# Fused attention and mixer on one Trainium2 core: third batch's query tails and fourth batch's queries loaded at other places of one queue

## The chip, the cores and the metric

The kernel runs on one core of a Trainium2 chip. A core has a matrix engine (PE; PEld is its weight load), a vector engine (DVE), an activation engine (ACT), a general engine (POOL) and an engine that mostly issues transfers (SP, SyncE), each with an instruction stream of its own that it works through in order. Sixteen DMA engines move data between HBM and the on-chip memory. The metric is the device time of one execution in microseconds (us), as the median of several runs.

## The reference

Eight batches of 8 heads, 576 positions, 64 elements a head. A linear attention with cosine and sine features is followed by a token and channel mixer:

```python
q_p = phi(q, cos_w, sin_w)          # relu(x)*cos, relu(x)*sin: 64 -> 128 features
k_p = phi(k, cos_w, sin_w)
kv = einsum('bhsf,bhsd->bhfd', k_p, v)
z = sum(k_p, axis=2)
num = einsum('bhsf,bhfd->bhsd', q_p, kv)
den = einsum('bhsf,bhf->bhs', q_p, z)[..., None] + 1e-06
x = (num / den), heads side by side: (8, 576, 512)
u = x + (relu(x^T @ w_tok1) @ w_tok2)^T      # over positions, 576 -> 256 -> 576
out = u + relu(u @ w_ch1) @ w_ch2            # over channels, 512 -> 1536 -> 512
```

## The kernel before

**Tiling.** The 576 positions of a batch are four chunks of 128 (0 to 3) and a tail of 64. The tails of two batches with numbers 2n and 2n+1 share one tile of 128 rows, called chunk R (its number is 4). Each batch loads three 1 MB tiles (qt, kt, vt, 128 partitions with 1 KB pieces) and tails qtt, ktt, vtt (128 KB each, 64 partitions, 256-byte pieces). For batch 2 the tails of batches 2 and 3 are both loaded, so that each of its tail tiles takes two transfers.

**Stages.** For each batch a `Front` makes the features (`k_side`, `q_side`, L263, on DVE), casts the values into v_aug (`values`, L274, on ACT), sums keys times values on PE (`kv`, L320) and copies the result out (`kv_out`, L331: one half on ACT, one on DVE, tile kv_sb). The query features are turned by a DMA transpose that SP issues (`q_trans_dma`, L350: qp to qpT, qp_tail to qpT_tail). `num` (L359) multiplies them with kv_sb; DVE divides (L367 to L369). The token mixer (`tok1` L382, `tok2` L406) gives u, which ACT casts (L413) and SP turns (L438, L443). A `Channel` then does the channel mixer: `c_main` (L546) and `c_tail` (L566) into h1T, `o_step` (L579) into the output tiles o_sb (L584), which SP stores (L586, L590).

**The order is written out by hand.** PE runs the steps of `Channel` of batch b one after the other: 12 steps for the channel matmuls (step 0 to 11), then the output steps, two matmuls each. Between them the work of batch b+1 is put at given steps: `pieces` returns a plan of (step, what, chunk). A negative step lies that many steps before the end of the loop before, among the last output steps there. What the plan puts there goes in that order into the streams of all engines. So the fronts of batches 2 and 3 are made in the loops of batches 1 and 2, and their pieces at negative steps at the end of the loops of batches 0 and 1.

**Loads.** `load_batch` puts transfers into SP's stream at the place where it is called: main tiles, tails, or both. All go through one SP queue, together with the stores and the transposes. An SP transfer waits, before it is issued, for the one eight places earlier to land, for its data, and for its buffer. kt, qt, vt and the tails have two buffers each.

The three flags of `pieces`: `first` is batch 1, `odd` are batches 1, 3, 5, 7, `late` is batch 2 alone. Lists that concern the change:

- batch 2: casts of the values at steps 6, 6, 7, 7, 7; K features of chunks 0 to 3 at -4, -3, 0, 1, Q features at 1, 2, 3, 4, K tail at 5, Q tail at 6; kv at 7, 7, 8, 8, 8 and kv_out at 8; num from step 10 on in the order 0, 1, 2, R, 3.
- batch 3, as odd: K and Q features of chunk 0 at -4 and -3, the others at steps 0 to 2; kv at 2 to 6, kv_out at 6, num from step 8 on. Its Q tail is the other half of batch 2's and is made with that.

SP's order before in the two stages (x2 is two transfers):

- batch 2: uT x2, uT_tail, vt(2), ktt x2, qtt x2, vtt x2, store x2, qpT 0 to 3, qpT_tail, kt(3), vt(3), qt(3), store x2
- batch 3: uT x2, kt(4), ktt x2, tail store x2, store, qpT 0, store, qpT 1 to 3, vt(4), vtt x2, qt(4), qtt x2

Of the kernel before, what the change touches and what calls it, by code (L numbers as in the profile page):

```python
# [16 lines left out]
def kernel(  # L17
# [17 lines left out]
    B, H, S, D = q.shape  # L35
# [11 lines left out]
    NCH = D_ch // P  # L47
# [30 lines left out]
    def after(later, earlier):  # L78
        tc.add_manual_dep(later.ins, earlier.ins.name,
                          mybir.DependencyInfo(mybir.DependencyClass.Sync,  # L80
                                               mybir.DependencyReason.DATA),
                          reason="order of the first loads")


    def load_main(dst, src, b, lo=0, hi=H, eng=nc.sync):
        return eng.dma_start(
            out=dst[:, lo:hi, 0:R * D].rearrange("p h (r d) -> p h r d", r=R),
            in_=src[b, lo:hi, 0:SM, :].rearrange("h (p r) d -> p h r d", r=R))


    def load_tail(dst, src, b, eng=nc.sync):
        return eng.dma_start(out=dst[half(b % 2)],
                                 in_=src[b, :, SM:S, :].rearrange("h s d -> s h d"))

    def tiles():
        return tuple(io.tile([P, H, R * D], F32, name=n) for n in ("qt", "vt", "kt"))

    def tail_tiles():
        return tuple(io.tile([P, H, D], F32, name=n) for n in ("qtt", "vtt", "ktt"))
# [116 lines left out]
    class Front:  # L216
# [244 lines left out]
        def pieces(self, b, before):  # L461

            first, odd, late = b == 1, b % 2 == 1, b == 2
            V, KV, N = self.values, self.kv, self.num
            KS, QS, QT, T = self.k_side, self.q_side, self.q_trans, self.tok2
            C, O = 0, NCH
            if first:

                u, act, pool = before.tok2, nc.scalar, nc.gpsimd
                plan = [(4, KS, 0), (4, KS, 1), (5, u, 0, ps_at, False), (5, KS, 2, True),
                        (6, KS, 3, True), (6, u, 1, ps_at, False), (7, KS, R), (7, V, R, nc.vector), (8, V, 0, act),
                        (8, V, 2, pool), (8, load_w_ch2, 0), (8, V, 3, pool),
                        (8, load_w_ch2, 1), (8, load_w_ch2, 2),
                        (8, u, 2, None, False), (9, V, 1, act), (9, u, 3, None, False),
                        (9, QS, 0), (10, u, R, None, False)]
                plan += [(11, KV, ci) for ci in range(NSC)]
                plan += [(11, QS, 1), (11, QS, 2), (11, self.kv_out),
                         (11, QT, 0, (0, H), act, ps_at), (11, QT, 1), (11, QS, R),  # L480
                         (O, QT, 2), (O, N, 0), (O, QS, 3), (O + 1, QT, R),
                         (O + 1, N, 1), (O + 3, N, 2), (O + 3, QT, 3),
                         (O + 5, N, R), (O + 7, N, 3), (O + 8, before.tail_cast)]
            else:
                plan = [(C + at, V, ci, nc.scalar)
                        for ci, at in enumerate((6, 6, 7, 7, 7) if late else (-1, -1, 0, 1, 2))]

                if odd:
                    sides = ((-4, KS, 0), (-3, QS, 0), (0, KS, 1), (0, KS, 2), (1, QS, 1),
                             (1, KS, 3), (1, QS, 2), (2, QS, 3))  # L490
                elif late:
                    sides = ((-4, KS, 0), (-3, KS, 1), (0, KS, 2), (1, KS, 3), (1, QS, 0),
                             (2, QS, 1), (3, QS, 2), (4, QS, 3), (5, KS, R), (6, QS, R))
                else:
                    sides = ((-4, KS, 0), (-3, KS, 1), (0, KS, 2), (1, KS, 3), (1, QS, 0),
                             (2, KS, R), (2, QS, 1), (3, QS, 2), (4, QS, R), (5, QS, 3))
                for at, side, ci in sides:
                    plan.append((C + at, side, ci))
                    if side == QS:
                        plan.append((C + at, self.q_trans_dma, ci))  # L500

                plan += [(C + at, KV, ci) for ci, at in
                         enumerate((7, 7, 8, 8, 8) if late else
                                   (2, 3, 4, 5, 6) if odd else (2, 3, 4, 6, 7))]
                plan.append((C + (8 if late else 6 if odd else 7), self.kv_out))
            if first:
                at, mix, t = (), O + 7, O + 11
            elif odd:
                at, mix, t = (C + 8, C + 9, C + 10, C + 11, O + 2), O + 3, O + 7
            elif late:  # L510
                at, mix, t = (C + 10, C + 11, O + 1, O + 2, O + 4), O + 5, O + 9
            else:
                at, mix, t = (C + 9, C + 10, C + 11, O + 1, O + 3), O + 4, O + 8
            plan += [(i, N, ci) for i, ci in zip(at, ORDER)]
            plan += [(mix, self.mix_head, 0), (mix + 1, self.mix_head, 1),
                     (mix + 2, self.mix_tail)]

            plan += [(t + at, T, ci) for ci, at in enumerate((0, 1, 2, 3, 3) if not first else
                                                             (0, 0, 1, 2, 2))]
            plan += [(t + 3 - first, self.u_trans_dma, 3, R)]  # L520
            plan.append((t + 2 - first, self.u_trans_dma, 0, 3))
            if odd:
                plan.append((t + 3 - first, self.tail_trans_dma))
            slots = {}
            for slot, what, *args in sorted(plan, key=lambda p: p[0]):
                slots.setdefault(slot, []).append((what, args))
            return slots
# [186 lines left out]
    def load_batch(b, which="kvq", behind=None, main=True, tails=True):  # L714
        if b not in io_tiles:
            io_tiles[b] = tiles()
        if b // 2 not in io_tails:
            io_tails[b // 2] = tail_tiles()
        qt, vt, kt = io_tiles[b]
        qtt, vtt, ktt = io_tails[b // 2]  # L720
        done = []
        for n in which:
            dst, tail_dst, src = {"k": (kt, ktt, k), "v": (vt, vtt, v), "q": (qt, qtt, q)}[n]
            if main:
                done.append(load_main(dst, src, b))
            if behind is not None and len(done) == 1:
                after(done[0], behind)
            if tails and b % 2 == 0:
                load_tail(tail_dst, src, b)
            if tails and (b % 2 == 0 or b == 1):  # L730
                load_tail(tail_dst, src, b | 1)
        return done
# [4 lines left out]
    tails = {0: tail0}  # L737
    fronts = {0: Front(0, results[0], tail0)}

    def next_front(b):  # L740
        if b // 2 not in tails:
            tails[b // 2] = Tail(b // 2)
        fronts[b] = Front(b, results[b], tails[b // 2])
        return fronts[b].pieces(b, fronts[b - 1])
# [3 lines left out]
    for b in range(B):  # L748
        if b > 0:
            c = Channel(b, results[b], tails[b // 2])  # L750
        steps = c.steps(AHEAD if b == 0 else 0)
        following = {}
        for i, step in enumerate(steps):
            step()
            for what, args in slots.pop(i, ()):
                what(*args)


            if b == 0 and i == NCH:
                load_batch(2, "kq", behind=w_ch2_done[1], tails=False)  # L760
            if b == 0 and i == NCH + 13:
                load_batch(2, "v", tails=False)
                load_batch(2, "kqv", main=False)
            if b == 1 and i == 9:
                load_batch(3, "kvq")
            if 1 < b < B - 2 and i == NSC:
                load_batch(b + 2, "vq")
            if 0 < b < B - 3 and i == NCH + 12:
                load_batch(b + 3, "k")
            if i == len(steps) - 4 and b + 2 < B:  # L770
                following = next_front(b + 2)
            for what, args in following.pop(i - len(steps), ()):
                what(*args)
        assert not slots
        slots = following
# [32 lines left out]
```

## Time and profile before

| what | value |
|---|---|
| median of 3 runs | 270.0 us (269.47 to 270.21) |
| the profiled execution, its own time | 270.61 us |
| its span, first to last instruction | 268.8 us |
| mean granted clock of PE | 1.000 |
| DMA | 53.68 MB in 91815 packets, mean 200 GB/s |
| qpT transposes, median from issue to landing | 4.3 us |
| qtt loads, median from issue to landing | 5.3 us |
| stores of 256 KB, median from issue to landing | 2.9 us |

The span leaves out 1.8 us around the program. Times in the timelines count from the start of the span; a row gives start and length in us, then engine, line and operation, the tiles as out<-in, and in square brackets the idle time of that engine before it with what ended it. SPq rows are issues: their length is how long SP was busy issuing, not how long the transfer took. A landing is the time at which the transfer's semaphore told of its end.

### The profile page before, as it was taken

How to read it: one execution, taken by the hardware profiler on the slowest of the kernel's cores; microseconds unless marked ns; L12 is line 12 of the kernel's file. 1: busy time of each engine (PE TensorE's matmuls, PEld its weight loads, DVE VectorE, ACT ScalarE, POOL GpSimd, SP SyncE). 2: the span in 40 equal slices, each digit the busy share in tenths (PEclk: the TensorE clock that was granted, in tenths of full speed). 3: DMA queues.
4: the chain of work that ended last, by engine and by line, in shares of the span. 5: the costliest groups of instructions: out<-in, count | busy, mean ns of one | idle time of the engine just before them, and what ended most of it. 6: DMA issues, size and time to landing. Idle time of an engine off the chain costs nothing.

```text
span 268.8 us, 5101 instructions
## 1 busy us (share of the span) xinstructions
PE 260.0 (97%) x2029; PEld 139.2 (52%) x2050; DVE 164.9 (61%) x376; ACT 129.9 (48%) x228; POOL 10.9 (4%) x24
## 2 busy tenths in 40 slices
PE   7989999999999999999999999999999999999994
PEld 2565465455544455446644455446644455445543
DVE  6874798794366747777466747776565846720022
ACT  4954975528606272446606372546606362526400
POOL 6300220000000000000000000000000000000000
PEclk9999999999999999999999999999999999999999
DMA  6999999589999999469984989189974580180032
GB/s 217 342 277 275 333 162 285 211 210 253 179 316 289 251 208 319 146 166 266 182 307 117 287 207 355 54 179 254 229 261 117 156 120 0 53 202 3 2 107 88
DMA packets 91815, 53.68 MB, mean 200 GB/s; under 512 B 59408, under 2 KB 86928, under 8 KB 91792
## 3 DMA queue, kind: packets, MB, share of 16 engines
q1 hardware_dynamic: 88432, 49.62, 69.5%
q0 software_dynamic: 2832, 3.21, 7.2%
q10 hardware_dynamic: 528, 0.52, 0.6%
q8 instruction: 16, 0.26, 0.4%
q14 instruction: 7, 0.06, 0.1%
HBM read 35.85 MB, written 9.44 MB: 168 GB/s over the span
## 4 chain that ended last, share of the span: by engine, by line
PE 86%; DVE 6%; DMA 3%; ACT 3%; issue 1%; DVEq 0%; ACTq 0%
PE o_ps L579 33%; PE c_ps L546 25%; PE u_ps L406 7%; PE b_ps L382 6%; PE ct_ps L566 3%; PE kv_ps L320 3%; PE num_ps L359 3%; DVE x_sb L369 3%; DMA qt<-in_q_dram 2%; DVE qp L263 1%; ACT h1T L550 1%; PE qT_ps L340 1%; DMA qpT_tail<-qp_tail 1%; PE idle_ps L204 1%; ACT v_aug L274 1%; PE c_ps L556 1%
## 5 line engine op out<-in xcount | busy, mean ns | idle before, releaser
L579 PE MATMUL o_ps<-w_ch,h1T 128*128 128x512 bf16 (+1 forms) x380 | 92.6, 372 | 0.6
L546 PE MATMUL c_ps<-uT,w_ch 128*128 128x512 bf16 (+2 forms) x384 | 92.2, 372 | 0.1
L550 ACT ACTIVATE h1T<-c_ps 128x512 bf16<-128x512 f32 x93 | 55.5, 599 | 60.5 <-PE c_ps L546 60.1
L579 PEld LDWEIGHTS <-h1T 128*128 128x128 bf16 x396 | 37.3, 98 | 39.5 <-issue 0.2
L546 PEld LDWEIGHTS <-w_ch 128*128 128x128 bf16 x384 | 33.5, 97 | 29.5 <-issue 0.2
L584 DVE TENSOR_TENSOR o_sb<-o_ps,u_sb 128x512 f32<-128x512 f32 (+1 forms) x33 | 22.3, 674 | 29.5 <-PE o_ps L579 29.4
L409 DVE TENSOR_TENSOR u_sb<-u_ps,x_sb 128x512 f32<-128x512 f32 x32 | 21.7, 689 | 6.0 <-PE u_ps L406 5.6
L413 ACT CAST u_bf<-u_sb 128x512 bf16<-128x512 f32 x28 | 17.3, 620 | 16.7 <-DVE u_sb L409 16.7
L406 PE MATMUL u_ps<-B,w_tok 128*128 128x512 bf16 x79 | 22.4, 379 | 0.2
L387 ACT ACTIVATE B<-b_ps 128x512 bf16<-128x512 f32 x8 | 4.8, 598 | 33.7 <-PE b_ps L382 33.5
L369 DVE TENSOR_TENSOR x_sb<-num_ps,den 128x512 bf16<-128x512 f32 x28 | 19.4, 691 | 1.0
L566 PEld LDWEIGHTS <-w_ch 128*128 128x128 bf16 x192 | 14.0, 98 | 9.2
L382 PE MATMUL b_ps<-x_sb,w_tok 128*128 128x512 bf16 x63 | 17.7, 379 | 0.1
L263 DVE TENSOR_SCALAR kp<-kt,cos_t 128x512 bf16<-128x512 f32 x32 | 15.2, 481 | 3.8 <-DMA kt<-in_k_dram 3.8
L566 PE MATMUL ct_ps<-uT_tail,w_ch 128*128 128x128 bf16 x192 | 17.2, 219 | 0.0
L274 ACT CAST v_aug<-vt 128x512 bf16<-128x512 f32 (+1 forms) x30 | 16.8, 587 | 0.1
L263 DVE TENSOR_SCALAR qp<-qt,cos_t 128x512 bf16<-128x512 f32 (+1 forms) x35 | 15.9, 455 | 0.5 <-DMA qt<-in_q_dram 0.5
L263 DVE TENSOR_SCALAR qp<-qt,sin_t 128x512 bf16<-128x512 f32 (+1 forms) x35 | 15.9, 455 | 0.0
L359 PEld LDWEIGHTS <-qpT 128*128 128x128 bf16 x256 | 11.5, 98 | 6.1 <-issue 1.1
L584 DVE TENSOR_TENSOR o_sb<-o_ps,u_tail 128x512 f32<-128x512 f32 x4 | 2.8, 692 | 19.0 <-PE o_ps L579 19.0
L359 PE MATMUL num_ps<-kv_sb,qpT 128*128 128x65 bf16 x256 | 13.0, 193 | 1.3 <-DVE x_sb L369 0.5
L331 DVE CAST kv_sb<-kv_ps 128x260 bf16<-128x260 f32 x8 | 3.5, 433 | 16.6 <-ACT kv_sb L331 16.5
(93 smaller groups left out, 228.6 us busy)
## 6 DMA issues: line engine op xcount, KB each, us to landing
out_dram<-o_sb SPq DMA_DIRECT2D x31, 256.0 KB, 2.9
kt<-in_k_dram SPq DMA_DIRECT2D x7, 1024.0 KB, 6.6
vt<-in_v_dram SPq DMA_DIRECT2D x7, 1024.0 KB, 6.6
qt<-in_q_dram SPq DMA_DIRECT2D x7, 1024.0 KB, 8.4
w_ch<-in_moe_w_ch_dram POOLq DMA_DIRECT2D x4, 384.0 KB, 10.2
w_ch<-in_moe_w_ch_dram POOLq DMA_DIRECT2D x3, 512.0 KB, 7.5
out_dram<-o_sb SPq DMA_DIRECT2D x10, 128.0 KB, 2.3
qtt<-in_q_dram SPq DMA_DIRECT2D x8, 128.0 KB, 5.3
```

Of the source, the lines that this page charges most:

```text
L263: nc.vector.tensor_scalar(o_ap, i_ap, scalar1=w, scalar2=0.0, op0=ALU.mult, op1=ALU.max)
L274: nc.scalar.copy(dst, src)
L359: nc.tensor.matmul(num_ps[:, g, j * DP:j * DP + D1], self.qT_of(ci, h), self.kv_sb[g][:, j, 0:D1], start=True, stop=True)
L369: nc.vector.tensor_mul(self.x_of(ci)[rows].rearrange("p (g j d) -> p g j d", g=2, j=HH), nv[:, :, :, 0:D], den.to_broadcast([rows.stop - r ...
L382: nc.tensor.matmul(self.b1_ps[mi], w, self.x_of(ci), start=(ci == ORDER[0]), stop=(ci == ORDER[-1]))
L406: nc.tensor.matmul(u_ps, w_tok2[:, ki, ci * P:(ci + 1) * P], self.B1[:, ki, :], start=(ki == 0), stop=(ki == NT - 1))
L409: nc.vector.tensor_add(u, u_ps[rows], self.x_of(ci)[rows])
L546: nc.tensor.matmul(c_ps[:, lo:hi], w_ch1[:, ki, mi * P:(mi + 1) * P], uT[:, lo // P:hi // P, ki, :], start=(ki == 0), stop=(ki == NCC - 1))
L550: nc.scalar.activation(self.h1T[:, mi, :], c_ps, AF.Relu)
L566: nc.tensor.matmul(self.ct_ps[:, mi % R, :], w_ch1[:, ki, mi * P:(mi + 1) * P], self.tail.uT[:, ki, :], start=(mi % R == 0 and ki == 0), s ...
L579: nc.tensor.matmul(o_ps, h, w_ch2[:, ki, cols], start=ki == 0, stop=ki == NCH - 1)
L584: nc.vector.tensor_add(o_sb, o_ps, u)
```

## The change

It moves loads and features; what is computed, and PE's order of instructions, stay the same.

1. Batch 2's casts of values stand at steps 5, 6, 6, 7, 7: those of chunks 0 and 2 are one step earlier.
2. Batch 2's late loads in the loop of batch 0 are vt, vtt, ktt; qtt moves to step 3 of the loop of batch 1, where it stands behind the transposes of batch 2's chunks 0 to 2.
3. Batch 3's qt is loaded near the end of the loop of batch 1, behind the transposes of batch 2's u, in the place where kt and ktt of batch 4 were; these move to step 1 of the loop of batch 2.
4. Batch 3 has a list of its own: K features of all chunks first (-4, -3, 0, 1), Q features with their transposes at steps 2, 3, 4, 5.

The last two lines of the diff keep the general rule for the later batches.

```diff
@@ -483,9 +483,12 @@
                          (O + 5, N, R), (O + 7, N, 3), (O + 8, before.tail_cast)]
             else:
                 plan = [(C + at, V, ci, nc.scalar)
-                        for ci, at in enumerate((6, 6, 7, 7, 7) if late else (-1, -1, 0, 1, 2))]
-
-                if odd:
+                        for ci, at in enumerate((5, 6, 6, 7, 7) if late else (-1, -1, 0, 1, 2))]
+
+                if b == 3:
+                    sides = ((-4, KS, 0), (-3, KS, 1), (0, KS, 2), (1, KS, 3),
+                             (2, QS, 0), (3, QS, 1), (4, QS, 2), (5, QS, 3))
+                elif odd:
                     sides = ((-4, KS, 0), (-3, QS, 0), (0, KS, 1), (0, KS, 2), (1, QS, 1),
                              (1, KS, 3), (1, QS, 2), (2, QS, 3))
                 elif late:
@@ -759,13 +762,19 @@
             if b == 0 and i == NCH:
                 load_batch(2, "kq", behind=w_ch2_done[1], tails=False)
             if b == 0 and i == NCH + 13:
-                load_batch(2, "v", tails=False)
-                load_batch(2, "kqv", main=False)
+                load_batch(2, "v")
+                load_batch(2, "k", main=False)
+            if b == 1 and i == 3:
+                load_batch(2, "q", main=False)
             if b == 1 and i == 9:
-                load_batch(3, "kvq")
+                load_batch(3, "kv")
+            if b == 1 and i == NCH + 12:
+                load_batch(3, "q")
+            if b == 2 and i == 1:
+                load_batch(4, "k")
             if 1 < b < B - 2 and i == NSC:
                 load_batch(b + 2, "vq")
-            if 0 < b < B - 3 and i == NCH + 12:
+            if 1 < b < B - 3 and i == NCH + 12:
                 load_batch(b + 3, "k")
             if i == len(steps) - 4 and b + 2 < B:
                 following = next_front(b + 2)
```

SP's order after, in the two stages:

- batch 2: uT x2, uT_tail, vt(2), vtt x2, ktt x2, store x2, qpT 0 to 2, qtt x2, qpT 3, qpT_tail, kt(3), vt(3), store x2
- batch 3: uT x2, qt(3), tail store x2, store x2, kt(4), ktt x2, qpT 0 to 3, vt(4), vtt x2, qt(4), qtt x2

On DVE the order in batch 2 is unchanged. In batch 3 it was K0, Q0, K1, K2, Q1, K3, Q2, Q3 (two instructions each) and becomes K0 to K3, Q0 to Q3. On ACT the casts of chunks 0 and 2 of batch 2 come one h1T earlier.

## The prediction

> **What bounds the kernel now.** I began with the page: TensorE (PE) is busy for nearly the whole span, so time can only come out of its pauses.
>
> ```profile
> PE 260.0 (97%) x2029; PEld 139.2 (52%) x2050; DVE 164.9 (61%) x376; ACT 129.9 (48%) x228; POOL 10.9 (4%) x24
> ```
>
> The step from one 128x512 matmul to the next is 216 ns. Going through the PE records for steps that are longer than their form's usual one, I find, behind the first 28 us and apart from single lost records, only the stretch from 59 to 75 us, where batch 2 is prepared between batch 1's channel matmuls. Its timeline on PE (start, length, engine, line):
>
> ```profile
> 65.04 0.92 PE L320 MATMUL kv_ps<-v_aug,kp 128*128 128x65 bf16 x16
> ...
> 70.62 0.42 PE L359 MATMUL num_ps<-kv_sb,qpT 128*128 128x65 bf16 x8 [0.44 <-ACT h1T L550]
> ...
> 74.57 0.42 PE L359 MATMUL num_ps<-kv_sb,qpT_tail 128*128 128x65 bf16 x8 [0.22 <-DMA qpT_tail<-qp_tail]
> ```
>
> The excess is 0.7 us in the kv matmuls (0.18, 0.28, 0.23, all behind ACT's casts to v_aug), 0.6 at 70.62, 0.4 at 74.57 and 0.24 at 59.43, the last in nothing that is edited. The list of waits names the DMA behind the second and third:
>
> ```profile
> PEld L359 <- DMA qpT_tail<-qp_tail: 0.7, 1, 0.7
> PEld L359 <- DMA qpT<-qp: 0.6, 1, 0.6
> ```
>
> So the change can win 1.7 us at most. Next I read what SP issues there, and what stands on DVE.
>
> ```profile
> 56.51 0.58 SPq L86 DMA_DIRECT2D vt<-in_v_dram  x1
> 57.15 1.31 SPq L92 DMA_DIRECT2D ktt<-in_k_dram  x2
> 58.50 2.02 SPq L92 DMA_DIRECT2D qtt<-in_q_dram  x2
> 60.57 2.00 SPq L92 DMA_DIRECT2D vtt<-in_v_dram  x2
> 62.67 1.04 SPq L586 DMA_DIRECT2D out_dram<-o_sb  x2
> 63.81 7.74 SPq L350 DMA_TRANSPOSE qpT<-qp  x4
> 71.64 1.26 SPq L350 DMA_TRANSPOSE qpT_tail<-qp_tail  x1
> ```
>
> ```profile
> 64.24 0.49 DVE L263 TENSOR_SCALAR qp_tail<-qtt,cos_t 128x512 bf16<-128x512 f32 x1
> 64.64 0.48 DVE L263 TENSOR_SCALAR qp_tail<-qtt,sin_t 128x512 bf16<-128x512 f32 x1
> 68.46 0.43 DVE L331 CAST kv_sb<-kv_ps 128x260 bf16<-128x260 f32 x1 [3.34 <-ACT kv_sb L331]
> ```
>
> The reader should see two things. SP is a backlog: the first turned queries go out at 63.81 although qp of chunk 0 was ready at 59.6. And on DVE the two features of the query tail stand directly ahead of kv_sb, which num of chunk 0 needs; the order of DVE around them is the same in both kernels. The queue's pace, by windows (stretch, length, busy times; clock, DMA share and GB/s last):
>
> ```profile
> 61.00:63.50 2.50, 2.50 (x19) 1.37 (x18) 1.19 (x4) 1.52 (x4) 0.00 (x0) 1.00 1.23 287
> ...
> 66.50:68.00 1.50, 1.43 (x31) 1.16 (x30) 0.00 (x0) 1.50 (x4) 0.00 (x0) 1.00 0.35 26
> ...
> 69.00:70.40 1.40, 1.18 (x10) 0.53 (x7) 0.00 (x0) 1.40 (x3) 0.00 (x0) 1.00 0.75 7
> ```
>
> Twice the queue all but stops: after two output stores that stand before transposes, and just after a 16 KB packet of the instruction queue at 68.72.
>
> **What is taken away.** The pair of qtt leaves the front of SP's queue: 60.57 - 58.50 = 2.07 us of issue, and 256 KB at 287 GB/s = 0.9 us of data. qpT of chunk 0, which landed at 70.57, lands 0.9 to 2.1 earlier: the 0.6 goes. vtt before ktt, and ACT's casts one step earlier, take away the 0.7. ktt now lands about 0.9 later; kp_tail then ends near 65.1 against its reader at 67.60, so 2.5 us of PE work hide that.
>
> **What is added in batch 2.** The qtt pair now stands behind qpT of chunks 0, 1 and 2. That third transpose was issued at 68.16 and landed 4.3 us later, at 72.45. Ahead of the last byte of qtt there are now the same transfers that were then ahead of the last byte of that transpose (vt, six tails, two stores, three transposes), so by the data qtt lands at 72.4. By issue, SP is through the third transpose 2.07 earlier than 70.20, at 68.1; the second tail goes out at about 69.0 (0.63 to 1.35 each) and lands at 71.4 if it takes the 2.4 of an unhindered store. Ends: 70.0 (71.4 and one 1.4 us stop avoided) and 74.3 (72.4 and one more stop of the longer kind, 1.9). I take 72.4, as data and not issue set the landings here.
> DVE stands still on qp_tail until then. Behind it wait kv_sb and every division of the num steps; behind kv_sb wait num of chunk 0 and all of PE. From landing: 0.05 + 0.88 (two features, 0.40 from start to start) + 0.43 (kv_sb) + 0.08 = 1.45, so num starts at 73.9 instead of 70.62: +3.3 (70.0 gives +0.9, 74.3 gives +5.1). This swallows both the 0.6 and the 0.7, which lie before it. qpT_tail is issued at 73.3 and lands 2.9 later, at 76.2; its reader comes 3.6 after num of chunk 0, at 77.5: the 0.4 is won. **Batch 2: +2.9 (+0.5 to +4.7).**
>
> **What is added in batch 3.** The stage of before on SP, and PE's first num there:
>
> ```profile
> 87.47 0.57 SPq L86 DMA_DIRECT2D kt<-in_k_dram  x1
> ...
> 91.12 0.54 SPq L586 DMA_DIRECT2D out_dram<-o_sb  x1
> 91.80 2.41 SPq L350 DMA_TRANSPOSE qpT<-qp  x1
> ```
>
> ```profile
> 100.03 0.41 PE L359 MATMUL num_ps<-kv_sb,qpT 128*128 128x65 bf16 x8
> ```
>
> The place at 87.47 now belongs to batch 3's queries. They land 6.6 us on (as kt did), at 94; DVE reaches them at 93.4 and has its last query feature near 97.2 instead of 96.7, before kv_sb at 99.16: hidden, with 2 us of cover. But batch 4's keys and their two tails now go out behind both stores, the second of which waits for o_sb at 91.93, so at 92.5, and all four transposes of batch 3 stand behind them. From the issue of kt to the landing of the first transpose took 9.8 in this stage (87.47 to 97.28) and 8.9 in batch 5's (147.19 to 156.12), with three stores in between worth 1.3 that now go first: 92.5 + 8.9 - 1.3 = 100.1 to 101.0. The reader is at 100.03, where it had 2.75 us of room. So 0.1 to 1.0, and 1.5 more if the stop at 99.8 to 101.2 (16 GB/s, after an instruction packet at 99.38 that comes with PE's own count, which is unchanged) finds this transpose in flight. I take 1.5 of 0.1 to 2.5, since its data would pass from 99.1 on. The later chunks follow 1.0 apart, and num asks 1.1 apart. vt and qt of batch 4 go out some 3.5 us later than 99.63 and are read at 114.79 and 120.9: hidden.
>
> **Sum.** +2.9 + 1.5 = +4.4 on the span of 268.8, or 270.61 + 4.4 = 275.0 for the profiled execution, which is 0.6 above the median of the runs, 270.0. Forecast: 274.4. PE's order is the same in both kernels, so no work is added.
>
> [...] If the tails did pass the transposes, they would land at 71.4, and the sum would be 273.4.
>
> **Rivals.**
> *PE's clock falls.* PE would stand from 69.4 to 73.9, 4.5 us; the longest pause after the start was 0.6, at a clock of 1.00 in every window. The price from rows: PE's first matmuls, from 1.38 to 4.2 us, are 427 ns apart instead of 216, in all 1.4 us lost. 274.4 + 1.4 = 275.8. Against it: nothing after the start shows a drop.
> [...]
>
> *Batch 2 alone pays.* qpT of batch 3 lands by 100.1 and no stop hits it: 270.0 + 2.9 = 272.9. For it: only 0.1 separates it from its reader at the low end.
>
> *Batch 3 alone pays*, the tails landing near 69.6, where loss and gain of batch 2 cancel: 270.0 + 1.0 to 1.5, 271.2. It needs both stops gone (72.45 - 2.9).
>
> *The other side: the tails come in time.* SP runs ahead of the data, so that qtt has landed by 67.5 (68.46 less 0.93) and kv_sb doesn't wait; then 1.7 is won and batch 3 costs at least 0.1: 268.4. It decides at a landing of 69.6. For it: the queue idled for 2.9 us between 66.5 and 70.4. Against it: without that idling the same bytes are through at 69.6, not before.
>
> **Chances.** Forecast 0.40, clock 0.18, batch 2 alone 0.17, batch 3 alone 0.10, in time 0.15. A measurement here tells 0.3%, 0.8 us, from no change: 269.2 to 270.8. Faster 0.13 (most of the last), within 0.07 (its rest, and half of batch 3 alone), slower 0.80. The range, 270.7 to 277.2, runs from the two low ends (+0.6) to the two high ends (+7.2) and takes in the clock's 275.8; the last rival stays outside.
>
> **What would show it.** Right: DVE's qp_tail waits some 7 us for qtt; PE waits over 3 us at num of batch 2, put down to kv_sb; the pauses at kv are gone; in batch 3 PE waits for qpT of chunk 0. Wrong: qtt landing before 69.6, or PE going through 70 us without a pause; then the forecast falls with its largest term. A clock under 1.00 after the pause speaks for the first rival.

## The result, and the profile after

| | before | after |
|---|---|---|
| median | 270.11 us (269.47 to 270.24, 4 runs) | 279.40 us (277.70 to 280.01, 4 runs) |
| ratio after to before, 95% interval | | 1.0339 [1.0286, 1.0392] |
| profiled execution, its own time | 270.61 us | 280.01 us |
| its span | 268.8 us | 278.2 us |
| mean granted clock of PE | 1.000 | 0.988 |

The changed kernel is 9.3 us slower. Every ratio in this document leaves out runs that lie more than 1.5% above the fastest of their kernel; this matters in one experiment only, `tails_back`, where two of four runs are left out and the ratio is therefore lower than its median says.

The page of the profile after, its line of busy times and the rows of PE and its clock over 40 slices of the span (7 us each):

```profile
PE 265.4 (95%) x2050; PEld 141.1 (51%) x2050; DVE 164.7 (59%) x376; ACT 129.8 (47%) x228; POOL 11.0 (4%) x24
...
PE   8989999999699995999999999999999999999994
...
PEclk9999999999799997999999999999999999999999
```

PE's instructions are the same, yet it is busy 5.4 us longer (a part of that is only that the profile of before lacks the records of 21 matmuls), and it stands idle more as well. Both happen in two places: slices 11 and 16 have a 6 and a 5 in PE's row, and the clock has a 7 in slice 11 and in slice 16. These are batch 2's and batch 3's num. The list of waits on PE (who waited, for whom; total, times, longest):

```profile
PE num_ps L359 <- DMA qpT<-qp: 3.3, 1, 3.3
PE num_ps L359 <- DVE kv_sb L331: 3.0, 2, 2.7
```

(Of the 3.0 for kv_sb, 0.3 lies in batch 0, as before.) The same two places in PE's timeline:

```profile
70.87 0.28 PE L359 MATMUL num_ps<-kv_sb,qpT 128*128 128x65 bf16 x4
73.81 0.38 PE L359 MATMUL num_ps<-kv_sb,qpT 128*128 128x65 bf16 x4 [2.66 <-DVE kv_sb L331]
```

```profile
107.76 0.60 PE L359 MATMUL num_ps<-kv_sb,qpT 128*128 128x65 bf16 x8 [3.33 <-DMA qpT<-qp]
```

In batch 2 four of the eight heads of chunk 0 go out at 70.87 with the half of kv_sb that ACT copied; the other four wait 2.66 us for the half that DVE copies. In batch 3 the wait is on the transfer itself. What DVE did before it came to its half of kv_sb:

```profile
72.53 0.49 DVE L263 TENSOR_SCALAR qp_tail<-qtt,cos_t 128x512 bf16<-128x512 f32 x1 [6.56 <-DMA qtt<-in_q_dram]
72.94 0.48 DVE L263 TENSOR_SCALAR qp_tail<-qtt,sin_t 128x512 bf16<-128x512 f32 x1
73.33 0.42 DVE L331 CAST kv_sb<-kv_ps 128x260 bf16<-128x260 f32 x1
```

It stood 6.56 us on the query tails, which had been sent behind three transposes. What SP issued for batch 2:

```profile
61.52 1.71 SPq L589 DMA_DIRECT2D out_dram<-o_sb  x2
63.34 4.28 SPq L350 DMA_TRANSPOSE qpT<-qp  x3
67.67 1.97 SPq L92 DMA_DIRECT2D qtt<-in_q_dram  x2
69.73 1.30 SPq L350 DMA_TRANSPOSE qpT<-qp  x1
73.44 1.23 SPq L350 DMA_TRANSPOSE qpT_tail<-qp_tail  x1
```

And for batch 3:

```profile
91.33 0.58 SPq L86 DMA_DIRECT2D qt<-in_q_dram  x1
92.01 1.19 SPq L593 DMA_DIRECT2D out_dram<-o_sb  x2
93.61 2.93 SPq L589 DMA_DIRECT2D out_dram<-o_sb  x2
96.59 0.43 SPq L86 DMA_DIRECT2D kt<-in_k_dram  x1
97.07 1.70 SPq L92 DMA_DIRECT2D ktt<-in_k_dram  x2
98.89 10.20 SPq L350 DMA_TRANSPOSE qpT<-qp  x4
```

The times from issue to landing in that stretch (operation, count, size, us):

```profile
qt<-in_q_dram SPq DMA_DIRECT2D x1, 1024.0 KB, 6.5
kt<-in_k_dram SPq DMA_DIRECT2D x1, 1024.0 KB, 8.1
...
qpT<-qp SPq DMA_TRANSPOSE x1, 8.8
```

Batch 4's kt, issued at 96.59, lands at 104.7, and the first transpose, issued at 98.89, lands at 107.7: 11.1 us behind the issue of kt.

Windows cut at the points where PE's clock changed (stretch, length, busy us of PE, PEld, DVE, ACT, POOL with instructions; then granted clock, DMA share, GB/s):

```profile
70.28:73.69 3.42, 0.87 (x11) 0.54 (x10) 1.16 (x3) 1.16 (x3) 0.00 (x0) 1.00 0.84 174
73.69:77.11 3.41, 3.30 (x23) 2.18 (x23) 1.12 (x4) 0.60 (x1) 0.00 (x0) 0.50 0.56 117
...
104.42:107.83 3.41, 0.08 (x3) 0.07 (x3) 0.00 (x0) 0.60 (x1) 0.00 (x0) 1.00 0.93 130
107.83:111.24 3.41, 3.41 (x23) 1.76 (x24) 1.69 (x6) 0.60 (x1) 0.00 (x0) 0.50 0.83 190
```

Behind each of the two waits PE worked at half its clock for 3.41 us, in which 512-column matmuls are 427 ns apart instead of 216.

Laying PE's weight loads of the two profiled executions side by side, one by one, gives the account: the difference between the start times of the same instruction, and where it grows.

| place | after against before, us |
|---|---|
| head, up to 44 us (waits for weights at the start and in batch 0's output steps) | +0.98 |
| batch 2: kv's pauses | -0.19 |
| batch 2: wait for qpT of chunk 0 | -0.59 |
| batch 2: wait for kv_sb | +2.86 |
| batch 2: half clock | +1.50 |
| batch 2: wait for qpT_tail, with what follows it | -0.32 |
| batch 3: wait for qpT of chunk 0 | +3.51 |
| batch 3: half clock | +1.59 |
| end (the rest of the run differs by less than 0.1) | +9.40 |

The first row is not the change's: nothing edited runs there, and the profiles of the experiments below, which have the same code there, show -0.3 to +0.8 in it.

### The profile page after: what moved, and what is told of

It reads as the page before. It is cut to its first block, busy times and chain, and to the rows that moved or that the text cites. A ratio compares the mean times of both kernels' runs of the same rounds, so it can differ in the third digit from the quotient of the medians.

```text
span 278.2 us, 5123 instructions
## 1 busy us (share of the span) xinstructions
PE 265.4 (95%) x2050; PEld 141.1 (51%) x2050; DVE 164.7 (59%) x376; ACT 129.8 (47%) x228; POOL 11.0 (4%) x24
## 4 chain that ended last, share of the span: by engine, by line
PE 72%; DMA 20%; SPq 4%; DVE 1%; POOL 1%; issue 1%; POOLq 0%; ACT 0%; DVEq 0%
PE o_ps L582 31%; PE c_ps L549 22%; DMA w_ch<-in_moe_w_ch_dram 7%; PE b_ps L382 5%; PE u_ps L406 5%; DMA vt<-in_v_dram 4%; PE ct_ps L569 3%; DMA qpT<-qp 3%; PE num_ps L359 3%; DMA kt<-in_k_dram 3%; PE kv_ps L320 2%; DMA ktt<-in_k_dram 2%; DMA qtt<-in_q_dram 1%; SPq L92 1%; SPq L86 1%
## 5 line engine op out<-in xcount | busy, mean ns | idle before, releaser
L549 PE MATMUL c_ps<-uT,w_ch 128*128 128x512 bf16 (+2 forms) x384 | 94.4, 379 | 0.1
L582 PE MATMUL o_ps<-w_ch,h1T 128*128 128x512 bf16 (+1 forms) x396 | 94.1, 372 | 0.2
L549 PEld LDWEIGHTS <-w_ch 128*128 128x128 bf16 x384 | 34.0, 99 | 30.5 <-issue 1.9
L359 PE MATMUL num_ps<-kv_sb,qpT 128*128 128x65 bf16 x256 | 13.8, 197 | 6.8 <-DMA qpT<-qp 3.3
L569 PEld LDWEIGHTS <-w_ch 128*128 128x128 bf16 x192 | 14.6, 101 | 9.5 <-issue 0.6
L359 PEld LDWEIGHTS <-qpT 128*128 128x128 bf16 x256 | 12.1, 101 | 12.2 <-issue 4.6
L569 PE MATMUL ct_ps<-uT_tail,w_ch 128*128 128x128 bf16 x192 | 17.9, 225 | 0.0
L367 DVE TENSOR_SCALAR den<-num_ps 128x8 f32<-128x8 f32 (+1 forms) x35 | 5.8, 165 | 16.5 <-PE num_ps L359 16.2
```

Of the source, the lines that this page charges most:

```text
L359: nc.tensor.matmul(num_ps[:, g, j * DP:j * DP + D1], self.qT_of(ci, h), self.kv_sb[g][:, j, 0:D1], start=True, stop=True)
L549: nc.tensor.matmul(c_ps[:, lo:hi], w_ch1[:, ki, mi * P:(mi + 1) * P], uT[:, lo // P:hi // P, ki, :], start=(ki == 0), stop=(ki == NCC - 1))
L569: nc.tensor.matmul(self.ct_ps[:, mi % R, :], w_ch1[:, ki, mi * P:(mi + 1) * P], self.tail.uT[:, ki, :], start=(mi % R == 0 and ki == 0), s ...
L582: nc.tensor.matmul(o_ps, h, w_ch2[:, ki, cols], start=ki == 0, stop=ki == NCH - 1)
```

## The experiments

My theory after this reading: two waits that have nothing to do with each other, one for each half of the change, and each long enough to bring down PE's clock. In batch 2 the query tails come late, and kv_sb stands behind their features in DVE's order. In batch 3 the first transpose stands behind batch 4's keys and tails in SP's queue, and these behind four stores. The rivals: that batch 3's wait is an echo of batch 2's delay; that the two halves only hurt together; that the half clock is a sign of the waits and costs nothing of its own; and that the casts and the pair vtt do harm as well. The diffs are against the changed kernel. "Both back" means that the third batch's query tails and the fourth batch's keys and queries are loaded and prepared as in the kernel before.

### Each half alone

`tails_back` puts batch 2's query tails back; batch 3's half of the change stays.

```diff
             if b == 0 and i == NCH + 13:
                 load_batch(2, "v")
-                load_batch(2, "k", main=False)
-            if b == 1 and i == 3:
-                load_batch(2, "q", main=False)
+                load_batch(2, "kq", main=False)
```

> Batch 2's query tails go back in front of the stores and the turned queries; all else as in the changed kernel. Theory (two waits of their own, each with a fall of PE's clock behind it): the wait for kv_sb in batch 2 and its clock loss go, batch 3's wait of 3.5 us and its clock loss of 1.6 stay, so 270.1 + 5.1 = 275.2, with one stretch of clock under 1.00. Rival (batch 3's wait is only the echo of batch 2's, whose pause pushes the queue back): both go, about 270.

Measured: 275.61 us (272.50 to 277.39, 4 runs), before 269.81; ratio 1.0138 [1.0085, 1.0190]. PE's longest wait in its profile:

```profile
PE num_ps L359 <- DMA qpT<-qp: 4.2, 1, 4.2
```

The whole of batch 3's wait is there without batch 2's delay, and in this profile it is longer, not shorter: the echo falls. The clock fell once, at 104.78, which cost 1.66 in the alignment. kt of batch 4 was issued at 92.37 and the first transpose landed at 104.34, 12.0 later. The profile is of the run of 276.65 us. The four runs took 272.50 at a mean clock of 1.000, 274.57 and 276.65 at 0.994 and 277.39 at 0.988; no trace tells how long the wait of the other three was.

`keys_back` puts batch 3's half back (its loads, its list of features, batch 4's keys) and leaves the query tails late.

```diff
-                if b == 3:
+                if False:
...
             if b == 1 and i == 9:
-                load_batch(3, "kv")
-            if b == 1 and i == NCH + 12:
-                load_batch(3, "q")
-            if b == 2 and i == 1:
-                load_batch(4, "k")
+                load_batch(3, "kvq")
...
-            if 1 < b < B - 3 and i == NCH + 12:
+            if 0 < b < B - 3 and i == NCH + 12:
```

> Batch 3's queries and batch 4's keys are loaded where they were, and batch 3's features have their old order; the query tails of batch 2 stay late. Theory: only batch 2's part is left: the wait for kv_sb of nearly 3 us, less the 0.6 and 0.3 won, plus 1.5 of clock, 270.1 + 3.3 = 273.4. Rival (echo): 273.4 as well; rival (no echo, but the tails cost only when qt of batch 3 is out of the queue): about 270.

Measured: 273.99 us (273.46 to 274.99, 4 runs), before 269.81; ratio 1.0159 [1.0129, 1.0189]. In PE's timeline the same split of the heads and the same wait:

```profile
70.04 0.29 PE L359 MATMUL num_ps<-kv_sb,qpT 128*128 128x65 bf16 x4
73.46 0.38 PE L359 MATMUL num_ps<-kv_sb,qpT 128*128 128x65 bf16 x4 [3.13 <-DVE kv_sb L331]
```

Aligned with before: +3.33 for kv_sb, +1.50 for one fall of the clock at 73.14, -0.59, -0.19 and -0.40 for the pauses that go. Batch 3 shows no wait. The two halves' medians lie 5.8 and 4.2 us above before, 10.0 together, and their ratios 1.4% and 1.6%, 3.0% together; both halves at once cost 9.3 us and 3.4%. Within the scatter of these few runs the two costs add.

### What is left of the change

`casts_only` puts both back and keeps ACT's earlier casts and vtt ahead of ktt.

```diff
-                if b == 3:
+                if False:
...
-                load_batch(2, "k", main=False)
-            if b == 1 and i == 3:
-                load_batch(2, "q", main=False)
+                load_batch(2, "kq", main=False)
...
-            if 1 < b < B - 3 and i == NCH + 12:
+            if 0 < b < B - 3 and i == NCH + 12:
```

> Both loads back; what is left of the change is the earlier casts of batch 2's values and vtt ahead of ktt and qtt. Theory: no wait over 0.7 us on PE behind the start, clock 1.00 throughout, 269.4 to 270.3 (the kv pauses shrink by 0.2 to 0.7). Rival (the casts or the order of the tails are at fault): over 272.

Measured: 269.76 us (269.25 to 270.77, 10 runs), before 269.81; ratio 1.0004 [0.9989, 1.0020]. In the alignment its profiled execution is 0.84 us ahead of before's (-0.18 at kv, -0.57 at the wait for qpT), but the medians are equal. So these parts do no harm. The pauses that the profile of before shows were in an execution that lay 0.6 above its median; whether the other executions have them is not known.

### The price of the clock

`filled` gives PE matmuls on zeros ahead of num's chunk 0, 30 of them in batch 2 and 36 in batch 3, as long as the two waits. They only keep PE busy: their results go to columns of num_ps that nothing reads.

```diff
-                busy(num_ps[:, 0, HH * DP:512], 1)
+                busy(num_ps[:, 0, HH * DP:512], fill)
...
-            plan += [(i, N, ci) for i, ci in zip(at, ORDER)]
+            fill0 = {2: 30, 3: 36}.get(b, 0)
+            plan += [(i, N, ci, fill0 if ci == ORDER[0] else 0) for i, ci in zip(at, ORDER)]
```

> The changed kernel with matmuls on a tile of zeros ahead of num of chunk 0 in batch 2 (30 of them) and batch 3 (36), into columns of PSUM that nothing reads; they add work that is not in the reference, and leave the result as it is. Theory (the array's clock falls because PE stands idle): clock 1.00 throughout, the two waits stay as they are, the 1.5 and 1.6 go: 279.4 - 3.1 = 276.3. Rival (the clock falls for another cause, or the fillers cost what they save): 279 or more.

Measured: 277.48 us (276.27 to 278.14, 4 runs), before 269.81; ratio 1.0279 [1.0246, 1.0311]. PE around batch 2's num, with the filling at L204:

```profile
69.88 2.64 PE L204 MATMUL num_ps<-zeros,ident 128*128 128x192 bf16 x30
72.36 0.29 PE L359 MATMUL num_ps<-kv_sb,qpT 128*128 128x65 bf16 x4
73.65 0.28 PE L359 MATMUL num_ps<-kv_sb,qpT 128*128 128x65 bf16 x4 [1.00 <-DVE kv_sb L331]
```

num goes on at 73.65, as late as without filling, and the clock is 1.00 throughout (1.000 in three of its four runs, 0.999 in the fourth). In the alignment the waits are still there (batch 2 +3.0, where the changed kernel has -0.59 + 2.86; batch 3 +3.15, where it has +3.51), and both half-clock terms are gone. So the half clock comes from PE's idling, and it has a price of its own. The size is a half miss: the median fell by 1.9 instead of 3.1. The profiled execution has the 276.3 that was expected, but by luck: against the changed kernel's it wins 3.1 for the clock and another 1.0 in the head, and the waits take 0.4 back. Where the other 1.2 of the median lies, I can't say; in an execution whose wait is shorter than the filling, the filling itself would hold num up, which no trace shows.

### Batch 2: the order on DVE, and the tails' place

Two kernels start from `keys_back`. `keys_back_qtail_behind_kv` leaves the tails as late as they are and puts their two features behind kv_sb in DVE's order.

```diff
-                              (2, QS, 1), (3, QS, 2), (4, QS, 3), (5, KS, R), (6, QS, R))
+                              (2, QS, 1), (3, QS, 2), (4, QS, 3), (5, KS, R), (9, QS, R))
```

> Batch 3's loads in their old place; the query tails of batch 2 stay late, but their two features stand behind the copy to kv_sb on DVE (three steps later) and not ahead of it. Theory (the tails cost because kv_sb and the divisions stand behind them in DVE's order): PE starts num of chunk 0 near 70 without a wait for kv_sb; DVE then stands on qp_tail ahead of the first division, and PE is held later, at the third num, where the buffers run out, so part of the loss comes back there: 271 to 273, against 274.0. Rival (the loss is the late turned queries themselves): 274 with the wait named DMA qpT.

Measured: 271.70 us (270.85 to 273.28, 8 runs), before 270.20; ratio 1.0066 [1.0041, 1.0091]. DVE, and then PE's waits:

```profile
68.72 0.43 DVE L331 CAST kv_sb<-kv_ps 128x260 bf16<-128x260 f32 x1 [3.31 <-ACT kv_sb L331]
72.19 0.48 DVE L263 TENSOR_SCALAR qp_tail<-qtt,cos_t 128x512 bf16<-128x512 f32 x1 [3.03 <-DMA qtt<-in_q_dram]
```

```profile
PE num_ps L359 <- DVE den L367: 0.9, 1, 0.9
PE num_ps L359 <- DMA qpT_tail<-qp_tail: 0.8, 1, 0.8
```

The tails land at 72.1, as in `keys_back`, but num of chunk 0 no longer waits and the clock stays up (in seven of the eight runs; the one with a mean of 0.993 is the slowest, 273.28). What remains are the divisions, which now stand behind the features, and the turned tail: two short waits instead of one long one. So the long wait came through DVE's order; what the late transfer costs without it is the two short waits.

`keys_back_tails_after_first` keeps the order on DVE and sends the tails behind the first transpose instead of the third.

```diff
-            if b == 1 and i == 3:
+            if b == 1 and i == 1:
                 load_batch(2, "q", main=False)
```

> Batch 3's loads in their old place; the query tails of batch 2 stand behind the first turned query chunk and not behind the third. Theory (PE's wait follows the landing of the tails, about 1 us for each transpose ahead of them): they land 2 us earlier, the wait for kv_sb falls from 3.1 to about 1, too short for the clock to fall: 270.3 to 271.5. Rival (any place behind a transpose costs the same): 274.

Measured: 270.74 us (269.21 to 271.33, 10 runs), before 270.20; ratio 1.0014 [0.9991, 1.0038]. The wait for kv_sb is 1.0 in PE's list instead of 3.1, the clock stays at 1.00; the tails land at 66.7 and 69.5.

`tails_first_behind_kv` has both edits.

> Both remedies for batch 2 at once, batch 3 as in the kernel before: the query tails go out behind the first transpose only, and their two features stand behind kv_sb on VectorE. If the wait of the changed kernel is the chain tails, then features, then kv_sb, nothing of it is left: num of batch 2 starts at about 70 without a wait for kv_sb, qp_tail is made while VectorE would wait anyway (the tails land at about 67 to 69.5, before kv_sb's copy at 68.5 to 69), the clock stays at 1.00, and the time is 269.0 to 269.9 (before about 270.0; of its pauses of 1.7 us in that stage up to 1.2 are won). The rival, that the transposes are delayed by the tails whatever DVE does, keeps 0.5 to 1 of a wait for qpT at num and gives 270.5 to 271.

Measured: 269.76 us (269.17 to 270.54, 11 runs), before 269.95; ratio 0.9987 [0.9974, 1.0001]. In batch 2's num, PE goes through chunk 0 in one piece without a wait, and one short wait is left:

```profile
70.44 0.41 PE L359 MATMUL num_ps<-kv_sb,qpT 128*128 128x65 bf16 x8
...
74.50 0.42 PE L359 MATMUL num_ps<-kv_sb,qpT_tail 128*128 128x65 bf16 x8 [0.33 <-DMA qpT_tail<-qp_tail]
```

Of batch 2's loss nothing is left that this measurement can tell, so tails behind one transpose need not cost anything. Whether it gains 0.2 or nothing is not told by an interval that reaches 1.0001. None of the kernels tried beats the kernel before for certain.

### Batch 3: where batch 4's keys stand

All start from `tails_back`. `tails_back_keys_behind` sends kt and ktt of batch 4 behind the four transposes, `tails_back_keys_early` sends them right behind qt, ahead of the four stores.

```diff
-            if b == 2 and i == 1:
+            if b == 2 and i == NSC:
                 load_batch(4, "k")
```

> Query tails in their old place, and batch 4's keys four steps later than in the changed kernel, so that the four turned queries of batch 3 go out ahead of them; batch 3's queries stay behind the turned u and its query features stay last. Theory (the keys that stand ahead of the turned queries make the wait): no wait for qpT in batch 3, clock 1.00, 269.5 to 270.5. Rival (the later load of batch 3's queries, or its later query features, make the wait): a wait of some 3 us stays, about 275.

```diff
             if b == 1 and i == NCH + 12:
                 load_batch(3, "q")
-            if b == 2 and i == 1:
                 load_batch(4, "k")
```

> Query tails in their old place; batch 4's keys go out right behind batch 3's queries, ahead of the four stores, so some 4 us earlier than in the changed kernel. Theory (the keys cost by how late the turned queries behind them land; the landing moves with the issue): the wait falls from about 4.2 us to 0 to 1.5, no fall of the clock, 269.8 to 271.5. Rival (any 1 MB more ahead of the turned queries costs the same): about 275.

`tails_back_tails4_behind` takes the order apart further: kt of 1 MB stays where the change put it, and only its two small tails go behind the transposes.

```diff
             if b == 2 and i == 1:
-                load_batch(4, "k")
+                load_batch(4, "k", tails=False)
+            if b == 2 and i == NSC:
+                load_batch(4, "k", main=False)
```

> As the kernel with the third batch's query tails put back (275.6, wait for qpT in batch 3 of 4.2 to 4.6, one fall of the clock), but of the fourth batch's keys only the 1 MB tile stays ahead of batch 3's transposes; its two small tails of 256-byte pieces go out behind them. There kt landed at 101.0, its tails at 102.9 and 103.1, the first transpose at 104.3. If each transfer ahead adds its own time to the wait, the first transpose lands 2.1 earlier (103.1 less 101.0), the wait falls to about 2.2, the clock stays at 1.00 and the time is 271.5 to 272.7. The rival, that the stop of the queue behind the instruction packet at about 100 us sets the landing whatever is ahead, keeps the wait above 3.5 and the time above 274. A second rival, that the tails are the whole of it, leaves a wait under 1 and 270.2 to 271.

What these measured, issue and landing from their profiled executions, the wait as PE's list has it:

| place of batch 4's kt, ktt | kt issued, landed | first transpose issued, landed | PE waits for qpT | time, us | ratio |
|---|---|---|---|---|---|
| behind four stores (`tails_back`) | 92.37, 101.04 | 95.04, 104.34 | 4.2 | 275.61 (272.50 to 277.39, 4 runs) | 1.0138 [1.0085, 1.0190] |
| kt there, ktt behind the transposes (`tails_back_tails4_behind`) | 91.82, 100.23 | 94.54, 102.67 | 3.1 | 274.64 (272.64 to 275.81, 4 runs) | 1.0143 [1.0077, 1.0208] |
| ahead of the stores (`tails_back_keys_early`) | 86.96, 95.13 | 94.07, 100.36 | 1.0 | 271.13 (270.26 to 272.43, 10 runs) | 1.0042 [1.0021, 1.0063] |
| behind the transposes (`tails_back_keys_behind`) | 100.90, 107.10 | 94.21, 96.95 | 0 here, 0.3 at the third num | 270.16 (269.21 to 273.13, 10 runs) | 1.0010 [0.9979, 1.0040] |

The last two are as expected, but for the 0.3 at the third num, and between them they show where the wait comes from: the first transposes are issued within 1 us of each other in all four kernels, but they land 2.7 to 9.3 after their issue, by what is ahead of them in the queue and by when that got in. With the keys behind them, nothing is lost that the interval can tell.

The second row missed both of its forecasts: the wait is neither 2.2 nor above 3.5. kt landed at 100.23, and what was then ahead of the transpose's end was this (windows of `tails_back_tails4_behind` while PE waits):

```profile
99.67:100.58 0.91, 0.00 (x0) 0.00 (x0) 0.00 (x0) 0.60 (x1) 0.00 (x0) 1.00 0.79 169
100.58:102.42 1.84, 0.00 (x0) 0.00 (x0) 0.00 (x0) 0.00 (x0) 0.00 (x0) 1.00 1.23 79
102.42:102.67 0.25, 0.00 (x0) 0.00 (x0) 0.00 (x0) 0.00 (x0) 0.00 (x0) 1.00 1.27 284
```

Nineteen of the packets of 256 bytes that were in flight from 100.58 to 102.42, and one of 16 KB from the instruction queue, took more than 0.5 us each, and the queue moved 79 GB/s; 0.25 after that the transpose landed. So between these two profiles taking the tails away saves about 1 us of the wait, and a stop of 1.84 keeps the rest. Such a stop with a 16 KB instruction packet in it also stands in the way of a transpose in `tails_back` (100.16 to 102.71, with 57 GB/s from 101 to 102), in `tails_back_keys_behind` (98.0 to 100.57, where it hit the third transpose) and in the changed kernel (105.69 to 107.46, at 90 GB/s). `tails_back_keys_early` has one too (98.80 to 100.10, at 12 GB/s), with its first transpose in flight, and waits only 1.0; so such a stop does not make the long wait by itself. That the packet causes the stop is argued from their coming together, and was not tried.

This kernel also shows the clock's price without filling: one of its four runs kept a clock of 1.000 and took 272.64, the three with a mean of 0.994 took 274.23 to 275.81.

## Why the prediction was wrong

The direction, both places and both releasers were right; the time, 274.4 with a range to 277.2, was 5.0 too low. Two steps failed. The sum put PE's clock at nothing, with its fall only as a rival beside it, and it fell behind both waits: +3.1 in the account above. And the landing of batch 3's first transpose came out too early, so that its wait was 2.0 longer than forecast. The rest is the head, +1.0, and batch 2 without its clock, 1.1 less.

**What is taken away.** The wait for qpT of chunk 0 went (-0.59), and qpT_tail's (-0.4, of which 0.1 came back). Of the 0.7 at kv only 0.19 came.

**What is added in batch 2: the mechanism right, the size 1.1 too large.** qtt was put at 72.4 and landed at 72.44; num was put at 73.9 and went on at 73.81. But this execution was 0.8 late from its head when it came there, with all its issues. `keys_back`, without that delay, went on at 73.46, so the landing was put some 0.3 to 0.4 too late (72.09 there); and I had missed that kv_sb has two halves, so that four of the eight heads go before the wait. Without the clock its net is 3.33 - 0.59 - 0.19 - 0.40 = +2.15, that of the changed kernel -0.19 - 0.59 + 2.86 - 0.32 = +1.8, where I had +2.9.

**What is added in batch 3: the step that took 8.9 to 9.8 from kt's issue to the first transpose's landing, less 1.3 for the stores.** That is 7.6 to 8.5; it measured 11.1, and 12.0 in `tails_back`, where kt was issued at 92.37, close to the 92.5 of the forecast. I had taken the time from a stage in which kt went out ahead of the stores, and subtracted the stores that no longer stood between. But the queue was not empty when kt got in: in `tails_back` batch 3's qt landed at 93.55 (my own forecast had it at 94), and the four stores landed between 93.86 and 96.85. So kt needed 8.7 from issue to landing, where it needed 6.6 before. From its landing to the transpose's it then took 3.3, where 3.2 - 1.3 = 1.9 was reckoned; a stop of the queue lies in that, which I had counted only as a chance between 0.1 and 2.5. The time of what is still in the queue was to be added, not taken off. SP also needed 5.3 us to issue that one transpose (5.8 in `tails_back`); what this adds to its landing is not shown. The wait was 3.5 where I took 1.5. `tails_back_keys_early`, with the same transfers but the keys ahead of the stores, waits 1.0, inside my 0.1 to 2.5: the forecast fits an order that the change does not have.

**The rival that came, twice: PE's clock falls.** I gave it 0.18, for batch 2 alone, at 1.4. It measured 1.50 there and 1.59 in batch 3, and `filled` shows that it hangs on the idling. What I held against it, that nothing after the start shows a drop, was no evidence: the longest pause in that trace was 0.6 us, and the forecast was of 4.5. As the runs show it, the fall is the consequence of a pause like the one forecast and not a case beside it. In the changed kernel each of the two falls lasts 3.413 us, and the second begins ten times that after the first (73.69 and 107.83); 0.87 us of PE work in the 3.41 us before the first did not prevent it.

**The other rivals.** Batch 2 alone and batch 3 alone are both refuted by the profile after, which has both waits; the two experiments with one half each show that one's wait and not the other's. The tails in time, the case on the other side, needed a landing by 67.5; even behind the first transpose the second tail lands at 69.5. The 273.4, the sum with tails that pass the transposes, is not borne out either: all 138 transfers of SP landed in the order of issue in the kernel before, in the changed kernel and in `tails_back`, and in the changed kernel the third transpose landed at 71.19 and the second tail, issued behind it, at 72.44.

**The range** allowed +7.2 for the two waits together. They came to 1.8 + 3.5 = 5.3, inside it only because batch 2's was small: batch 3's 3.5 lies outside its own 0.1 to 2.5. The clock stood in the range once, on top of the middle, and not on top of the high end or for a second pause. With 275.8 for the first rival, batch 3's 2.0 and a second fall at 1.6, the sum would have been 279.4. That this is the measured median is luck, since the head's +1.0 and batch 2's -1.1 cancel. Two slips in the working do not bear on the miss: the terms from landing to num add up to 1.44, which makes the low end +0.8 and not +0.9, and the two low ends as stated give 270.6 and not 270.7.

## What to carry to other kernels

Before a load is moved behind something else in a queue, look up the consumer's place in its engine's order: in `keys_back` DVE stood 6.5 us on the late tails, with the copy that PE waits for behind their two features, and moving these two short instructions behind the copy took most of the loss away (from 4.2 us above before to 1.5). The time from issue to landing belongs to the state of the queue at the time of issue; if the new place is behind transfers that have not landed, their time is to be added (kt's landing took 8.7 us here instead of 6.6), and a time from a stage with an emptier queue can't be taken over. And in the profiles here PE's clock fell behind each unfilled pause of 2.7 to 4.2 us, and behind none of about 1.0; so a forecast of a pause near 3 us in this kernel has to carry the clock's 1.5 to 1.7 us with it, once for every pause.

## What the runs showed that I had not expected

**The clock falls although PE works a little before.** Of the 3.41 us before each of five falls in four kernels PE worked 0.87 us (the changed kernel, 70.28 to 73.69), 0.08 (104.42 to 107.83), 0.61 (`keys_back`, 69.72 to 73.14), 0.39 (`tails_back`, 101.37 to 104.78) and 0.63 us (`tails_back_tails4_behind`, 99.93 to 103.35). The pause before the first of them, 2.66 us, is itself shorter than 3.41. Each fall then lasted 3.41 us and cost 1.5 to 1.7 us.

The clock's records in the changed kernel are 3.413 us long at half the clock, 30.720 at the full one and again 3.413 at half: one, nine and one of a step of 3.413. Laid out on the grid of these steps, the windows behind the start in all twelve profiles separate cleanly. All eight that held 1.31 us of PE work or less were followed by half the clock (three of them at the end of the program, where PE has finished), and none that held 1.54 or more was. The two windows nearest to the bound, both near the end of the program, are this one of `keys_back`, behind which the clock fell:

```profile
267.70:271.11 3.41, 1.31 (x12) 0.93 (x10) 0.85 (x2) 0.00 (x0) 0.00 (x0) 1.00 0.42 154
```

and this one of `keys_back_tails_after_first`, behind which it stayed:

```profile
263.43:266.84 3.41, 1.54 (x15) 1.13 (x12) 0.85 (x2) 0.00 (x0) 0.00 (x0) 1.00 0.42 154
```

So in these traces it counts how much PE works in a window, not whether it works at all. The ends of matmuls are modelled, which makes the bound rough, and no experiment was made to find it. A pause that the grid cuts in two can pass in part: in `tails_back` the window from 97.95 to 101.37 holds the first 1.2 us of the pause and 2.26 us of work, and the clock fell only behind the next. That may be why one of the four runs of `tails_back_tails4_behind` kept its clock, but that run has no trace.

**SP itself is held while it issues.** In the profile after, the transposes of batch 3 took 10.20 us to issue, the first 5.3 of them (rows of the operation, duration min, median, max in ns, first and last start):

```profile
L350 SPq DMA_TRANSPOSE qpT<-qp x1: 5295/5295/5295, 98.9 to 98.9; - x1
```

The one at 69.73 in the same profile, shown above, took 1.30. So the transposes behind it were late in their issue too, and so was every load behind them: vt of batch 4 is not reached before 109.14. The first of these issues took 5.8 in `tails_back` as well, and 1.3 in `tails_back_keys_early` and `tails_back_keys_behind`, where the keys don't stand right ahead of it; what holds SP there was not tried.
